# First tile of an attention and two-layer gated kernel: two weight blocks multiplied in plain fp32 instead of in split halves

## The chip, the cores and the metric

The kernel runs on one core of one Trainium2 chip. The metric is the device time of one execution in microseconds (us). Before the change three runs took 1025.25, 1028.63 and 1029.28 us (median 1028.63 us).

Engines are named as in the profile: PE is the matrix engine (PEld its weight loads), DVE the vector engine, ACT the scalar engine, POOL the general-purpose engine, SP the one that issues the DMAs.

## The reference

Three layers follow each other. Attention over keys and values that are averaged eight at a time, then two feed-forward layers with a product of two projections in the middle; 2304 tokens, 512 model columns, 1536 inner columns.

```python
# attention: k and v averaged over 8 neighbours, softmax(q k^T / 8) v
xn = x / sqrt(mean(x * x) + 1e-6) * rms_g
g = xn @ w_gate                      # 512 -> 1536
h = g * sigmoid(g) * (xn @ w_val)
x2 = h @ w_out                       # 1536 -> 512
out = ((x2 @ w_a) * (x2 @ w_b)) @ w_out2
```

All weights arrive as float64 and are turned into fp32 on the chip.

## The kernel before

The tokens of the first feed-forward layer are cut into five tiles (512, 256, 512, 512, 512 tokens), the 1536 inner columns into twelve weight blocks of 128. For each block and tile PE computes gate (`g`) and value (`v`), each as four matmul steps over the 512 model columns; ACT takes silu of the gate (line 812), DVE multiplies it by the value (`ht`, line 818), and PE adds the block's share of the output into four PSUM accumulators (`acc`, line 675). Of `g` and of `v` there is one PSUM bank each, so that a new gate waits for the silu of the last one, and a new value for the product `ht` of the last one.

A product of two fp32 tensors is made in one of two ways. *Split*: each operand is divided into a high part (rounded to fp32r, a cast on ACT) and a low part (the rest, a subtraction), and three fp32r matmuls per step give low x high, high x high and high x low. `split_w` (line 618) does it for a weight block: cast `wh` at line 621, subtraction `wl` at line 622 on POOL, or on DVE where the token carries an exclamation mark. `split_x` (line 625) does it for the tokens: cast `xh` at line 636, subtraction `xl` at line 637. *Direct*: one fp32 matmul per step on the operands as they are. The profile records one fp32 matmul as two. The output projection of the first tile and the whole second tile are direct (lines 675 and 654), everything else of the layers is split.

While the first tile is computed, the weights are still arriving. Each of the 36 weight parts of the first layer goes through a chain (`convert_steps`, line 575): DMA into one of four staging buffers `st`, two ACT operations (lines 590 and 591), two DVE operations (lines 597 and 600), one POOL addition (line 607). A staging buffer is free for the next DMA when the POOL addition is done. The attention of the first 512 tokens, the keys of the next batch (line 189, line 180) and the normalisation (a few small DVE operations at lines 478 to 493, then the scaling of x at line 529, once for each half of 256 tokens) run on the same engines.

In the first tile the first two weight blocks are computed in halves of 256 tokens, so that work can start when the first half of x is there. The jobs are numbered: jobs 0 and 1 are blocks 0 and 1 on the first half, jobs 2 and 3 the same blocks on the second half, jobs 4 to 13 are blocks 2 to 11 on all 512 tokens. What each engine does in which order is set by the table `FIRST` (line 32), a list of tokens that is worked off from left to right: `g2a` and `g2b` are the two halves of job 2's gate, `v2a`, `v2b` its value, `a2` its silu, `h2` its product `ht`, `o2` its output matmuls; `s3.1` splits part 1 (value) of block 3, `x0` and `x1` split the two halves of x, `c` converts a weight part, `l` loads one. A `-` or `=` ahead of a token puts its instructions behind the work listed before on its engine. After that a scheduler places the instructions; the order on each engine is fixed when the program is built.

Of the kernel before, what the change touches and what calls it, by code (L numbers as in the profile page):

```python
# [20 lines left out]
SLICE = 768  # L21
HALF = SLICE // 2
FINE = 2
DIRECT = 0

# [4 lines left out]
FIRST = """  # L32
=k0 -A0.0@att =k1 l -k2! k3 -l t0@att =A0.1@acc1 A0.2@att w0 =A0.5@acc0 =A0.6@acc3 =A0.7@acc3
-w1 A0.3 =A0.4 w2 t1 =A0.8 A1.0@att A1.1@acc0 A0.9! =c l =A1.2@v -V0.0@acc0 A1.5@acc2 -A1.3
-V0.1@acc1 c A1.6@acc3 s0.0 -V0.2@acc0,v A1.4! -V0.3@g,acc0 =A1.7@acc1 A1.8 A1.9 V0.4@acc2,att
=V0.5@att -c =V1.0@acc0 =V0.6 =V0.7@v =V1.1@g -x0! -g0a V1.2@att,acc3 =V1.3@acc2,acc1 c =g0b
-V1.4@acc0,att =l V1.5@acc2 =V1.6 =V1.7@acc0 s0.1! =c =x1 -a0 s1.0 =v0a =v0b -c =h0 =o0 -g1a
-g1b -s1.1! =c L0 -a1 A2.0 -g2a v1a =L1 -g2b p0 =p1! v1b =c s2.0! h1 =c =a2 =c g3a =c v2a =v2b
-h2 =c g3b =o1 a3 =p2 =o2 -v3a =v3b -s2.1 -h3 g4a g4b p3! -c a4 -v4a s3.0 =c -p4 -v4b s3.1! =c
=o3 =g5a =p5! =c =h4 c -c s4.0! -g5b -c -a5 s4.1! v5a -s5.0 v5b -h5 -g6a -o4 -g6b a6 -p6 -c  # L40
=v6a p7 -s5.1 =v6b -A2.1 -g7a -c =g7b -h6 =c =M0 -c =A2.2 =c -A2.3 =s6.1! =s6.0! -a7 o5 -c v7a
=c =A2.4 v7b s7.0! -h7 -g8a -g8b =a8 -o6 s7.1! c =v8a A2.5 c =s8.0 =p8 v8b =g9a -V2.0 g9b -h8
-a9 -o7 v9a =g10a -s9.0 v9b -c =s8.1 -h9 =c =V2.1 =o8 -V2.2 g10b =s9.1! -a10 -c V2.3 =v10a
-V2.4 -c v10b s10.0 g11a -g11b -h10 =a11 =V2.5 =c -s10.1 =c =o9 -g12a =c -v11a s11.0 =A3.0
=g12b -v11b h11 =a12 -V2.6 -v12a -g13a c -o10 A3.1 -v12b -o11 =g13b -s11.1 =A3.2 -A3.3 =M1
-h12 a13 -v13a -V2.7 -v13b =o12 -h13 =A3.4 =o13 =A3.5
""".split()
SECOND = """
A4.0 =r0 -r1 r2 -r3 r4 -r5 V3.0 r7 =r6 =r8 -V3.1 =V3.2 N0 =V3.3 A4.1 -N1
# [14 lines left out]
def attention_moe_moe2(  # L64
# [715 lines left out]
    def first_tile():  # L780
# [8 lines left out]
        def half(j, part, c0):  # L789
            f, cols, last = jobs[j]  # L790
            if f < DIRECT:
                terms = ((wf[0, f, part], xf_t[0]),)
# [529 lines left out]
```

## Time and profile before

| | us |
|---|---|
| median of three runs | 1028.63 |
| the profiled execution, its own time | 1028.68 |
| its span from the first to the last instruction | 1026.9 |
| PE busy in the span | 984.9 (96%) |
| DVE, ACT, POOL busy | 608.1, 437.9, 369.5 |

The profiled execution's time stands 1.8 us over its span and 0.05 us over the median. PE is busy nearly all the time from about 120 us on; in the first four of the page's forty slices (25.7 us each) it stands at 4, 9, 8 and 8 tenths, in the stretch in which the first weights are being converted. The split products of the first tile begin at 43.8 us.

### The profile page before, as it was taken

To read this page: it belongs to the slowest core of one execution; us is meant where nothing else is said; L and a number is where in the kernel's file an instruction comes from. 1 tells how busy PE (TensorE), PEld (TensorE's weight loads), DVE (VectorE), ACT (ScalarE), POOL (GpSimd) and SP (SyncE) were. 2 spreads that over 40 slices of the span, in tenths; PEclk is the share of its full clock that TensorE was granted. 3 is DMA by queue.
4 is the path that set the end of the run, shared out by engine and by line. 5 is a ranking of instruction groups with operands and counts; after the bars stand their busy time and mean duration, and the time that the engine had idled before them with its cause. 6 is when DMAs were issued, how large, how long until landed. Compare 5 with 4: busy or idle time off the path is not lost. (4 is left out here: it accounts for less than half of the span.)

```text
span 1026.9 us, 13276 instructions
## 1 busy us (share of the span) xinstructions
PE 984.9 (96%) x4820; PEld 845.0 (82%) x4820; DVE 608.1 (59%) x963; ACT 437.9 (43%) x822; POOL 369.5 (36%) x301
## 2 busy tenths in 40 slices
PE   4988999999999989999999999999999999999998
PEld 3776676778888877888788899999999998888886
DVE  6898966564733765363627759766776665322221
ACT  3845661232534545444445445434444434331211
POOL 6476672100153433443348620533344333310000
PEclk9889999999999999999999999999999999999999
DMA  8556543320100002000112133444443444643431
GB/s 227 156 175 194 178 140 105 102 78 1 41 1 21 1 1 62 1 1 1 41 28 75 42 111 113 139 148 135 140 151 125 130 129 178 203 140 118 139 113 72
DMA packets 82801, 101.53 MB, mean 99 GB/s; under 512 B 24112, under 2 KB 63024, under 8 KB 82736
## 3 DMA queue, kind: packets, MB, share of 16 engines
q1 hardware_dynamic: 82736, 100.69, 31.7%
q8 instruction: 38, 0.62, 0.2%
q14 instruction: 27, 0.22, 0.1%
HBM read 73.93 MB, written 26.74 MB: 98 GB/s over the span
## 5 line engine op out<-in xcount | busy, mean ns | idle before, releaser
L622 POOL TENSOR_TENSOR wl<-wf,wh 128x512 fp32r<-128x512 f32 x121 | 164.4, 1366 | 263.0 <-ACT wh L621 255.3
L621 ACT CAST wh<-wf 128x512 fp32r<-128x512 f32 x132 | 80.2, 619 | 76.2 <-PE acc L667 27.4
L1103 DVE TENSOR_TENSOR hl<-hf,hh 128x768 fp32r<-128x768 f32 x36 | 35.5, 992 | 95.1 <-ACT hh L1102 95.1
L1125 PE MATMUL o<-woh,hl 128*128 128x512 f32 x216 | 85.8, 397 | 0.0
L1125 PE MATMUL o<-woh,hh 128*128 128x512 f32 x216 | 85.0, 394 | 0.0
L1125 PE MATMUL o<-wol,hh 128*128 128x512 f32 x216 | 84.7, 392 | 0.0
L607 POOL TENSOR_TENSOR w<-w,st 128x512 int32<-128x512 int32 x24 | 31.9, 1330 | 116.0 <-DVE w L600 114.8
L1102 ACT CAST hh<-hf 128x768 fp32r<-128x768 f32 x36 | 29.8, 834 | 91.4 <-PE o L1125 81.5
L675 PE MATMUL acc<-ht,wf 128*128 128x256 f32 (+1 forms) x208 | 67.0, 465 | 1.2 <-DVE ht L818 0.7
L607 POOL TENSOR_TENSOR wf<-wf,st 128x512 int32<-128x512 int32 x36 | 52.9, 1475 | 39.0 <-DVE wf L600 17.3
L1240 ACT ACTIVATE ht<-g 128x512 f32<-128x512 f32 (+1 forms) x48 | 26.1, 544 | 92.8 <-PE g L654 90.2
L1248 DVE TENSOR_TENSOR ht<-ht,v 128x512 f32<-128x512 f32 (+1 forms) x48 | 29.6, 617 | 56.2 <-PE v L654 54.9
L667 PE MATMUL acc<-hh,wl 128*128 128x512 f32 x144 | 57.7, 400 | 3.5 <-ACT hh L1257 3.5
L654 PE MATMUL v<-xh,wl 128*128 128x512 f32 x144 | 57.9, 402 | 0.0
L667 PE MATMUL acc<-hl,wh 128*128 128x512 f32 x144 | 56.8, 394 | 0.1
L654 PE MATMUL g<-xh,wl 128*128 128x512 f32 x144 | 56.7, 394 | 0.0
L667 PE MATMUL acc<-hh,wh 128*128 128x512 f32 x144 | 56.6, 393 | 0.0
L654 PE MATMUL v<-xl,wh 128*128 128x512 f32 x144 | 56.3, 391 | 0.0
L654 PE MATMUL g<-xh,wh 128*128 128x512 f32 x144 | 56.2, 390 | 0.0
L654 PE MATMUL v<-xh,wh 128*128 128x512 f32 x144 | 56.1, 390 | 0.0
L654 PE MATMUL g<-xl,wh 128*128 128x512 f32 x144 | 56.1, 390 | 0.0
L1032 ACT COPY p<-X 128x384 f32<-128x384 f32 x36 | 17.3, 480 | 90.1 <-PE X L1024 90.1
(212 smaller groups left out, 2731.5 us busy)
## 6 DMA issues: line engine op xcount, KB each, us to landing
hf<-h SPq DMA_DIRECT2D x36, 384.0 KB
st<-in_moe_w_out_dram SPq DMA_DIRECT2D x24, 512.0 KB
h<-u SPq DMA_DIRECT2D x36, 192.0 KB
h<-p SPq DMA_DIRECT2D x36, 192.0 KB
st<-in_moe_w_gate_dram SPq DMA_DIRECT2D x12, 512.0 KB
st<-in_moe_w_val_dram SPq DMA_DIRECT2D x12, 512.0 KB
st<-in_moe_w_a_dram SPq DMA_DIRECT2D x12, 512.0 KB
st<-in_moe_w_b_dram SPq DMA_DIRECT2D x12, 512.0 KB
```

The costliest lines, as they stand in the source:

```text
L607: nc.gpsimd.tensor_tensor(out=bits, in0=bits, in1=low, op=ALU.add)
L621: nc.scalar.copy(wh, wf[ph, f, i])
L622: (nc.vector if boot["alt"] else nc.gpsimd).tensor_sub(wl, wf[ph, f, i], wh.bitcast(F32))
L654: nc.tensor.matmul(bank[:, :n], w[:, c, :], x[:, c, cols], start=(i == 0), stop=(i == len(terms) * KD - 1),)
L667: nc.tensor.matmul(accs[c][:, cols], w[:, c, :], x[:, :n], start=(f == 0 and i == 0 and cols.start == 0), stop=(f == NF - 1 and i == 2),)
L675: nc.tensor.matmul(accs[c][:, cols], wf[0, f, 2][:, c, :], ht[:, :cols.stop - cols.start], start=(f == 0 and cols.start == 0), stop=(f == ...
L1032: nc.scalar.copy(t, src[:, :HALF])
L1102: nc.scalar.copy(hh, hf)
L1103: nc.vector.tensor_sub(hl, hf, hh.bitcast(F32))
L1125: nc.tensor.matmul(accs[i], x[:, sub], y, start=(f == 0 and j == 0), stop=(f == NF - 1 and j == 2),)
L1240: act = nc.scalar.activation(out=ht[:, :m], in_=gb[:, :m], func=AF.Silu)
L1248: nc.vector.tensor_mul(ht[:, :m], ht[:, :m], vb[:, :m])
```

## The change

`DIRECT` goes from 0 to 2: gate and value of weight blocks 0 and 1 (jobs 0 to 3) are made directly, one fp32 matmul per step on `xf` and `wf`, in place of three fp32r matmuls. In the table the four tokens `s0.0`, `s0.1`, `s1.0`, `s1.1` (the splits of gate and value of these blocks) are taken out, and `x0!` and `x1`, which stood ahead of job 0's gate and among the tokens of job 0, now stand after job 2's silu, before block 2 needs them. The split of the output weights, of all other blocks and of all later tiles stays.

```diff
-DIRECT = 0
+DIRECT = 2
...
-=V0.5@att -c =V1.0@acc0 =V0.6 =V0.7@v =V1.1@g -x0! -g0a V1.2@att,acc3 =V1.3@acc2,acc1 c =g0b
+=V0.5@att -c =V1.0@acc0 =V0.6 =V0.7@v =V1.1@g -g0a V1.2@att,acc3 =V1.3@acc2,acc1 c =g0b
...
-g1b -s1.1! =c L0 -a1 A2.0 -g2a v1a =L1 -g2b p0 =p1! v1b =c s2.0! h1 =c =a2 =c g3a =c v2a =v2b
+A2.0 -g2a v1a =L1 -g2b p0 =p1! v1b =c s2.0! h1 =c =a2 =c -x0! g3a =c v2a =v2b =x1 -h2 =c g3b
```

The order on the engines moves at two places that matter below.

On PE, where the first gate begins (`g_401` and `v_513` before, `g_391` and `v_483` now, are gate and value of job 0; `kT` is a transpose for the next batch). Before:

```order
L434 MATMUL sq_1_413<-ones_100,sq_1_3_466 128x2 x2
L804 MATMUL g_401<-xh_395,wl0_288 128x256
L804 MATMUL g_401<-xh_395,wh0_287 128x256
L804 MATMUL v_513<-xh_395,wl1_494 128x256
L804 MATMUL v_513<-xh_395,wh1_493 128x256
L210 MATMUL kT_1_912<-ident_95,kp_1_605 128x72
L804 MATMUL g_401<-xl_396,wh0_287 128x256
L804 MATMUL g_401<-xh_395,wl0_288 128x256
```

Now:

```order
L434 MATMUL sq_1_399<-ones_100,sq_1_3_448 128x2 x2
L804 MATMUL g_391<-xf_0_292,wf0_0_0_240 128x256 x4
L804 MATMUL v_483<-xf_0_292,wf1_0_0_276 128x256 x4
L210 MATMUL kT_1_832<-ident_95,kp_1_543 128x72
L318 MATMUL sc_4_0_849<-KB0_106,qTs_4_528 64x144 x2
L804 MATMUL g_505<-xf_0_292,wf0_0_1_421 128x256
```

Gate and value of job 0 now stand as four matmuls each, in one piece, with the transpose behind them instead of among them.

On DVE, from the product `ht` of job 1 to that of job 2 (`ht_570` and `ht_642` before, `ht_520` and `ht_576` now). Before:

```order
L529 TENSOR_TENSOR xf_0_296<-xf_0_296,rb_1_490 128x4x256
L637 TENSOR_TENSOR xl_396<-xf_0_296,xh_395 128x2x256 x2
L818 TENSOR_TENSOR ht_570<-ht_570,v_590 128x256
L622 TENSOR_TENSOR wl0_630<-wf0_0_2_562,wh0_629 128x512
L597 TENSOR_SCALAR wf2_0_2_636<-wf2_0_2_636 128x512
L189 TENSOR_REDUCE kp_1_605<-kv_1_4_608 72x64
L600 SCALAR_TENSOR_TENSOR wf2_0_2_636<-st_0_2_2_526,wf2_0_2_636 128x512
L597 TENSOR_SCALAR wf0_0_3_646<-wf0_0_3_646 128x512
L818 TENSOR_TENSOR ht_642<-ht_642,v_667 128x256
```

Now:

```order
L622 TENSOR_TENSOR wl0_564<-wf0_0_2_512,wh0_563 128x512
L818 TENSOR_TENSOR ht_520<-ht_520,v_536 128x256
L597 TENSOR_SCALAR wf2_0_2_570<-wf2_0_2_570 128x512
L597 TENSOR_SCALAR wf0_0_3_580<-wf0_0_3_580 128x512
L600 SCALAR_TENSOR_TENSOR wf2_0_2_570<-st_0_2_2_488,wf2_0_2_570 128x512
L600 SCALAR_TENSOR_TENSOR wf0_0_3_580<-st_0_3_0_510,wf0_0_3_580 128x512
L637 TENSOR_TENSOR xl_587<-xf_0_292,xh_586 128x2x256 x2
L597 TENSOR_SCALAR wf1_0_3_597<-wf1_0_3_597 128x512
L637 TENSOR_TENSOR xl_587<-xf_0_292,xh_586 128x2x256
L600 SCALAR_TENSOR_TENSOR wf1_0_3_597<-st_0_3_1_555,wf1_0_3_597 128x512
L637 TENSOR_TENSOR xl_587<-xf_0_292,xh_586 128x2x256
L818 TENSOR_TENSOR ht_576<-ht_576,v_603 128x256
```

All four subtractions `xl`, two of which stood far earlier and two ahead of job 1's product, now stand between the products of jobs 1 and 2, with three conversions.

## Rows read from the trace of the kernel before

**Rows 1.** The page: busy time, share of the span and instructions of each engine.
```profile
PE 984.9 (96%) x4820; PEld 845.0 (82%) x4820; DVE 608.1 (59%) x963; ACT 437.9 (43%) x822; POOL 369.5 (36%) x301
```

**Rows 2.** Windows: stretch, length, busy us of each engine, granted clock, DMA.
```profile
43.78:58.65 14.87, 10.41 (x50) 8.86 (x50) 14.61 (x27) 8.01 (x15) 8.50 (x8) 0.73 0.53 158
58.65:76.62 17.97, 16.55 (x92) 14.84 (x92) 15.75 (x21) 10.93 (x20) 12.87 (x11) 0.87 0.56 180
76.62:116.44 39.82, 35.88 (x146) 25.91 (x147) 35.13 (x46) 23.09 (x39) 23.94 (x18) 0.96 0.64 199
116.44:1026.90 910.46, 894.39 (x4393) 772.60 (x4391) 510.59 (x807) 373.06 (x700) 299.80 (x229) 1.00 0.28 87
```

**Rows 3.** Timeline of PE: start, length, instruction, count, idle before it and releaser.
```profile
46.06 0.38 PE L210 MATMUL kT<-ident,kp 72*128 72x72 f32 x1 [1.06 <-DVE kp L189]
...
54.96 0.70 PE L472 MATMUL rb<-dg,ones 128*128 128x256 f32 x2 [1.99 <-DVE dg L464]
...
58.65 1.22 PE L675 MATMUL acc<-ht,wf 128*128 128x256 f32 x2 [0.52 <-DVE xf L529]
...
76.62 0.47 PE L804 MATMUL v<-xh,wl 128*128 128x512 f32 x1 [1.42 <-DVE ht L818]
...
86.86 0.64 PE L804 MATMUL v<-xh,wl 128*128 128x512 f32 x1 [2.77 <-DVE ht L818]
...
113.56 0.50 PE L804 MATMUL g<-xh,wl 128*128 128x512 f32 x1 [1.17 <-DVE wl L622]
```

**Rows 4.** Timeline of PE: split matmuls ten apart, first at 1.2, then at 2.4 GHz.
```profile
47.03 0.41 PE L804 MATMUL g<-xh,wl 128*128 128x256 f32 x1
...
49.17 0.41 PE L804 MATMUL v<-xh,wl 128*128 128x256 f32 x1
...
70.97 0.28 PE L804 MATMUL v<-xh,wh 128*128 128x256 f32 x1
...
72.17 0.28 PE L804 MATMUL v<-xl,wh 128*128 128x256 f32 x1
```

**Rows 5.** Timeline of PE: fp32 matmuls of 256 columns, at 1.2 and at 2.4 GHz.
```profile
26.63 1.91 PE L420 MATMUL xT<-ef,vm 128*128 128x256 f32 x4
28.34 0.45 PE L318 MATMUL sc<-KB,qTs 128*128 128x144 f32 x1
...
208.57 1.89 PE L654 MATMUL g<-xf,wf 128*128 128x256 f32 x8
210.30 0.38 PE L367 MATMUL eT<-ident,e 128*128 128x128 f32 x2
```

**Rows 6.** Timeline of DVE: the products `ht` of jobs 1, 2 and 4.
```profile
63.84 0.42 DVE L818 TENSOR_TENSOR ht<-ht,v 128x256 f32<-128x256 f32 x1 [1.56 <-PE v L804]
...
67.09 0.42 DVE L818 TENSOR_TENSOR ht<-ht,v 128x256 f32<-128x256 f32 x1
...
86.14 0.68 DVE L818 TENSOR_TENSOR ht<-ht,v 128x512 f32<-128x512 f32 x1
```

**Rows 7.** Groups of DVE from 63.8 to 94 us: count, busy us, mean ns.
```profile
L600 DVE SCALAR_TENSOR_TENSOR wf<-st,wf 128x512 int32<-128x512 int32 x11 | 12.9, 1174 | 0.2
L597 DVE TENSOR_SCALAR wf<-wf 128x512 int32<-128x512 int32 x11 | 9.0, 819 | 0.0
...
L189 DVE TENSOR_REDUCE kp<-kv 72x64 f32<-72x512 f32 x2 | 2.2, 1087 | 0.0
```

**Rows 8.** Timeline of DVE and POOL: the subtractions of x, and POOL beside one pair.
```profile
45.92 1.29 DVE L637 TENSOR_TENSOR xl<-xf,xh 128x512 fp32r<-128x512 f32 x2
...
59.28 3.01 DVE L637 TENSOR_TENSOR xl<-xf,xh 128x512 fp32r<-128x512 f32 x2 [0.69 <-ACT xh L636]
...
60.01 2.86 POOL L180 TENSOR_TENSOR kv<-kv 72x512 f32<-72x512 f32 x2
```

**Rows 9.** Timeline of DVE: a conversion's two operations with POOL idle.
```profile
33.57 0.42 DVE L597 TENSOR_SCALAR wf<-wf 128x512 int32<-128x512 int32 x1
34.02 0.69 DVE L600 SCALAR_TENSOR_TENSOR wf<-st,wf 128x512 int32<-128x512 int32 x1
```

More of the change, by code (lines that the diff above doesn't have):

```diff
@@ L34 @@
 -w1 A0.3 =A0.4 w2 t1 =A0.8 A1.0@att A1.1@acc0 A0.9! =c l =A1.2@v -V0.0@acc0 A1.5@acc2 -A1.3
--V0.1@acc1 c A1.6@acc3 s0.0 -V0.2@acc0,v A1.4! -V0.3@g,acc0 =A1.7@acc1 A1.8 A1.9 V0.4@acc2,att
-=V0.5@att -c =V1.0@acc0 =V0.6 =V0.7@v =V1.1@g -x0! -g0a V1.2@att,acc3 =V1.3@acc2,acc1 c =g0b
[L37 to L46, printed above, removed]
+-V0.1@acc1 c A1.6@acc3 -V0.2@acc0,v A1.4! -V0.3@g,acc0 =A1.7@acc1 A1.8 A1.9 V0.4@acc2,att
+=V0.5@att -c =V1.0@acc0 =V0.6 =V0.7@v =V1.1@g -g0a V1.2@att,acc3 =V1.3@acc2,acc1 c =g0b
+-V1.4@acc0,att =l V1.5@acc2 =V1.6 =V1.7@acc0 =c -a0 =v0a =v0b -c =h0 =o0 -g1a -g1b =c L0 -a1
+A2.0 -g2a v1a =L1 -g2b p0 =p1! v1b =c s2.0! h1 =c =a2 =c -x0! g3a =c v2a =v2b =x1 -h2 =c g3b
+=o1 a3 =p2 =o2 -v3a =v3b -s2.1 -h3 g4a g4b p3! -c a4 -v4a s3.0 =c -p4 -v4b s3.1! =c =o3 =g5a
+=p5! =c =h4 c -c s4.0! -g5b -c -a5 s4.1! v5a -s5.0 v5b -h5 -g6a -o4 -g6b a6 -p6 -c =v6a p7
+-s5.1 =v6b -A2.1 -g7a -c =g7b -h6 =c =M0 -c =A2.2 =c -A2.3 =s6.1! =s6.0! -a7 o5 -c v7a =c
+=A2.4 v7b s7.0! -h7 -g8a -g8b =a8 -o6 s7.1! c =v8a A2.5 c =s8.0 =p8 v8b =g9a -V2.0 g9b -h8 -a9
+-o7 v9a =g10a -s9.0 v9b -c =s8.1 -h9 =c =V2.1 =o8 -V2.2 g10b =s9.1! -a10 -c V2.3 =v10a -V2.4
+-c v10b s10.0 g11a -g11b -h10 =a11 =V2.5 =c -s10.1 =c =o9 -g12a =c -v11a s11.0 =A3.0 =g12b
+-v11b h11 =a12 -V2.6 -v12a -g13a c -o10 A3.1 -v12b -o11 =g13b -s11.1 =A3.2 -A3.3 =M1 -h12 a13
+-v13a -V2.7 -v13b =o12 -h13 =A3.4 =o13 =A3.5
 """.split()
```

## The prediction

> **What bounds the kernel now.** I read the page first, then the windows, then the timelines of PE and DVE where the windows show PE idle.
>
> The page shows PE busy for 96% of the span [rows 1]. The windows tell where the rest is: from 116.44 us to the end PE works 894.39 of 910.46 us, while in the three stretches from 43.78 to 116.44 us, where the first tile's split products stand, it works 62.8 of 72.7 us, and the granted clock is 0.73, 0.87 and 0.96 there [rows 2]. With two levels of the clock (1.2 and 2.4 GHz) a mean of 0.73 says that 54% of 14.87 us, 8.0 us, ran at 1.2 GHz, and 0.87 that 26% of 17.97 us did. The change works only in these stretches. Whatever it shifts at 116 us reaches the end nearly whole, since PE is the bound from there on; so the question is by how much PE gets past 116 us earlier or later.
>
> The timeline of PE names what it waits for in these stretches: keys on DVE (1.06 us at 46.06), the normalisation on DVE (1.99 us at 54.96, 0.52 us at 58.65), and the products `ht` and a `wl` on DVE (1.42, 2.77 and 1.17 us at 76.62, 86.86 and 113.56) [rows 3]. Each is DVE's. DVE is busy 14.61 of 14.87, 15.75 of 17.97 and 35.13 of 39.82 us there [rows 2]: until about 87 us the first tile runs at the pace of DVE's queue, not of PE. That decides how I count.
>
> **The change part by part.**
>
> *The products on PE.* At 1.2 GHz ten split matmuls take 2.14 us, at 2.4 GHz 1.20 us [rows 4]; a half tile's gate or value has twelve: 2.57 and 1.44 us. Direct it has four fp32 matmuls, eight records. Four records of that size take 1.71 us at 1.2 GHz (26.63 to 28.34), eight take 1.73 us at 2.4 GHz (208.57 to 210.30) [rows 5]: 3.42 and 1.73 us. So each of the eight products (gate and value of jobs 0 to 3) costs PE 0.85 us more at the lower level, 0.29 us at the higher: 2.3 us if all stand at 2.4 GHz, 6.8 us if none does, 4.6 us with half of them at each, as the clock of the first two stretches suggests. Where PE waits for DVE anyway this is hidden; it counts in full where a DVE operation waits for PE, which is the case at one point, job 1's `ht`.
>
> *What goes from ACT, POOL and DVE.* Four weight splits: four casts `wh` and two subtractions on ACT and POOL, two on DVE. ACT and POOL are busy for 8.01 and 8.50 of 14.87 us in the first stretch [rows 2], so I count nothing for theirs; if their queues carried the stretch, it would be up to their own 1 to 3 us, and that stands in the faster rival. On DVE one of its two subtractions and the first pair `xl` (1.29 us at 45.92 [rows 8]) stood ahead of the second half's scaling. A subtraction `wl` has the form of half such a pair, 0.65 us. So the scaling, and with it the second half of x on PE, comes 0 to 1.9 us earlier. I take 1.0, the middle, since job 0's `ht` also stands in DVE's queue there, and waits for PE products that are now longer.
>
> *Up to job 1's `ht`* (63.84 us; DVE had waited 1.56 us for PE [rows 6]). From 58.65 us PE had done one output matmul and twenty split matmuls for it, gate of job 2 and value of job 1 mixed; now the same place holds one output matmul and seven direct ones. At 1.2 GHz: 20 x 0.214 = 4.3 us against 7 x 0.855 = 6.0 us, 1.7 us more. With the 1.0 us from above, job 1's `ht` comes 0.7 us later (bounds -0.2 and +1.7).
>
> *From job 1's `ht` to job 2's.* This is where the moved split of x lands. Before, 3.25 us (63.84 to 67.09 [rows 6]). Now ten DVE operations stand ahead of job 2's `ht`: three L597, three L600 and four `xl`, after job 1's `ht` of 0.42 us. Bare, by 0.42 and 0.69 us [rows 9] and 0.645 us (half of the pair at 45.92 [rows 8]) this is 0.42 + 1.26 + 2.07 + 2.58 = 6.3 us. But beside POOL's work the same operations take longer: L600 1.17 and L597 0.82 us in the mean of the stage [rows 7], and a pair `xl` 3.01 us where POOL's two additions (2.86 us at 60.01) ran with it [rows 8]: 0.42 + 2.46 + 3.51 + 6.02 = 12.4 us. From both I take off 0.6 us: two operations of 0.69 us would take 1.38 and the pair takes 1.29, so that each starts about 0.08 us before the last one ends, at the seven that are not `xl`. Bounds 5.7 and 11.8 us. POOL is busy in about two thirds of the second and third stretch [rows 2], but two of its additions are gone too; I take 9.0 us, a little over the middle. So job 2's `ht` comes 5.7 us later against job 1's (2.5 to 8.5).
>
> The Trainium skill, in "GPSIMD Engine Reference" (1. Specifications), says that POOL and DVE share their SBUF interfaces, and that a DVE instruction with two SBUF inputs, or in a two-port mode, contends with POOL for them. The pair at 59.28 us agrees, at 3.01 against 1.29 us. By this rule every `xl` that meets a POOL addition waits, and this term would stand at its upper bound; without it at the lower.
>
> *From job 2's `ht` to job 4's.* Before 19.05 us (67.09 to 86.14 [rows 6]), in which DVE was the pace. In the new order two L600 and one L597 fewer stand there (they have moved ahead) and one more L189: -2 x 1.17 - 0.82 + 1.09 = -2.1 us by the means [rows 7], -0.7 us bare (0.69 and 0.42 [rows 9]). I take -1.9.
>
> *The sum.* Job 4's `ht`, for which PE waits at 86.86 us, comes 0.7 + 5.7 - 1.9 = 4.5 us later. PE alone would get there 4.6 us of work later, minus 1.06 us (job 0's gate and value no longer have the transpose and `xl` in their midst) and minus the waits of 1.42 and 2.77 us: -0.7 us. DVE comes later, so DVE decides. After that the work is the same; I let the wait of 1.17 us and the clock of the third stretch stand (0; -2.8 if both went, +1.7 for another 3.4 us at 1.2 GHz). 1028.68 + 4.5 = **1033.2 us**, against the profiled execution, which stands at the median.
>
> **The rivals.**
>
> *The bare queue.* DVE's new queue meets POOL seldom: -0.2 + 2.5 - 0.7 = +1.6, 1030.3 us. For it: POOL has two additions fewer, and DVE waits for PE before job 1's `ht`, time in which POOL can run ahead. Against: the means of rows 7 stand in just this stage.
>
> *Every subtraction collides.* +1.7 + 8.5 - 1.9 = +8.3, 1037.0 us. It decides as soon as POOL's `wl` subtractions of blocks 2 and 3 fall between jobs 1 and 2. For it: the pair of 3.01 us. Against: POOL would have to be busy without a break.
>
> *Faster, by PE as the pace.* If the weights get through DVE and POOL earlier by what is taken out, the queue is short when job 1 ends. Then the waits of 1.06, 1.42 and 2.77 us go, the slow part of the third stretch with them (8% of 39.82 us, 1.6 us lost), and the products cost 2.3 us at full clock: 2.3 - 1.06 - 1.42 - 2.77 - 1.6 = -4.6, 1024.1 us. It decides if job 4's `ht` comes by 86 us. For it: DVE loses 1.3 us of `wl` in all. Against: it keeps all four `xl` and gets them at its busiest place.
>
> **How the numbers follow.** A measurement of this kernel can tell 0.5%, 5.1 us, from no change. Forecast: 0.50, its own range 1030.7 to 1036.2, 0.20 of it above 1033.8. Bare queue 0.18, inside 0.5%. All colliding 0.22, slower. Faster 0.10, half of it by more than 0.5%. So slower 0.42, same 0.30 + 0.18 + 0.05 = 0.53, faster 0.05. The range takes in the bare queue, most of the colliding case and half of the faster one: 1027.2 to 1038.5 us.
>
> **What would show it.** Right: PE's gate and value of job 0 in one piece without the wait at 46 us; `ht` of job 1 within 2 us of 63.84; 7 to 11 us from there to job 2's `ht`, with `xl` pairs well over 1.3 us; a new wait of PE for that `ht` at its output matmuls; job 4's `ht` at about 90.6 us; the stretch after 116 us as long as before. Wrong: job 4's `ht` at 86 us or earlier, or PE without a wait for `ht` between 65 and 90 us (then the products alone are the cost), or a stretch after 116 us that gives the delay back.

## The result and the profile after

Twelve runs of the changed kernel took 1030.22 to 1038.05 us, median 1033.33; twelve of the kernel before, on the same chip, 1025.25 to 1029.73, median 1027.28. The ratio is 1.006, with a 95% interval of 1.0043 to 1.0077: 6 us slower. The profiled execution took 1031.21 us with a span of 1029.3, 2.1 us under its median. The forecast said 1033.2 us.

By the page PE is busy for 984.1 us of the span, before for 984.9 [rows 1]. The windows of the same first three stretches (answers [rows 2]; columns as there):

```profile
43.78:58.65 14.87, 11.53 (x41) 8.81 (x41) 14.28 (x26) 8.32 (x15) 9.72 (x9) 0.81 0.57 173
58.65:76.62 17.97, 14.14 (x56) 11.04 (x55) 14.54 (x18) 9.98 (x19) 11.74 (x9) 0.91 0.46 147
76.62:116.44 39.82, 36.25 (x156) 26.14 (x155) 35.24 (x49) 21.58 (x36) 26.11 (x18) 1.00 0.68 205
```

PE is busy for 14.14 us of the second stretch, before for 16.55. Its waits (answers [rows 3]):

```profile
53.48 1.56 PE L675 MATMUL acc<-ht,wf 128*128 128x256 f32 x6 [1.86 <-DVE ht L818]
...
56.52 0.70 PE L472 MATMUL rb<-dg,ones 128*128 128x256 f32 x2 [1.49 <-DVE dg L464]
...
68.63 0.50 PE L804 MATMUL g<-xh,wl 128*128 128x512 f32 x1 [1.05 <-ACT ht L812]
...
70.26 0.50 PE L804 MATMUL g<-xl,wh 128*128 128x512 f32 x1 [0.90 <-DVE xl L637]
...
72.89 3.45 PE L675 MATMUL acc<-ht,wf 128*128 128x256 f32 x8 [1.89 <-DVE ht L818]
...
88.90 0.50 PE L804 MATMUL v<-xh,wl 128*128 128x512 f32 x1 [1.57 <-DVE ht L818]
...
115.19 0.50 PE L804 MATMUL g<-xh,wl 128*128 128x512 f32 x1 [0.99 <-DVE wl L622]
```

The wait for keys at 46 us is gone. New are waits for job 0's `ht` (1.86), for the silu that frees the gate's bank (1.05, at job 4's first gate matmul), for an `xl` (0.90) and for job 2's `ht` at its output matmuls (1.89); these last three make 3.84 us. At job 4's `ht` PE waits 1.57 us, before 2.77.

DVE's timeline, the products of jobs 1, 2 and 4 (answers [rows 6]) and the subtractions `xl` (answers [rows 8]):

```profile
62.51 0.42 DVE L818 TENSOR_TENSOR ht<-ht,v 128x256 f32<-128x256 f32 x1 [3.43 <-ACT wf L590]
...
64.72 3.47 DVE L637 TENSOR_TENSOR xl<-xf,xh 128x512 fp32r<-128x512 f32 x2
...
71.82 0.68 DVE L637 TENSOR_TENSOR xl<-xf,xh 128x512 fp32r<-128x512 f32 x1
72.42 0.41 DVE L818 TENSOR_TENSOR ht<-ht,v 128x256 f32<-128x256 f32 x1
...
88.17 0.68 DVE L818 TENSOR_TENSOR ht<-ht,v 128x512 f32<-128x512 f32 x1
```

From job 1's to job 2's product it now takes 9.91 us, before 3.25, and an `xl` takes 0.68 us at 71.82 but 3.47 for the pair at 64.72, with POOL at work. Job 4's product comes 2.0 us later than before.

The next view wasn't among the rows of before: DVE in the normalisation of the second half, four of its small operations on four columns that met POOL, one that did not (46.26), and `dg`, and under them POOL in the same time. Job 0's product stands among them at 53.01.

```profile
46.26 0.15 DVE L491 TENSOR_TENSOR by<-br 128x4 f32<-128x4 f32 x1
...
46.67 1.24 DVE L492 TENSOR_TENSOR by<-by,ba 128x4 f32<-128x4 f32 x1
...
48.84 1.26 DVE L491 TENSOR_TENSOR by<-br 128x4 f32<-128x4 f32 x1
...
50.63 2.46 DVE L492 TENSOR_TENSOR by<-by,ba 128x4 f32<-128x4 f32 x1
...
54.00 1.54 DVE L492 TENSOR_TENSOR by<-by,ba 128x4 f32<-128x4 f32 x1
...
56.00 0.47 DVE L464 TENSOR_SCALAR dg<-ident,br 128x128 f32<-128x128 f32 x2
...
46.48 1.41 POOL L607 TENSOR_TENSOR wf<-wf,st 128x512 int32<-128x512 int32 x1 [6.56 <-DVE by L491]
48.65 1.43 POOL L607 TENSOR_TENSOR wf<-wf,st 128x512 int32<-128x512 int32 x1 [0.75 <-ACT st L591]
50.05 1.79 POOL L180 TENSOR_TENSOR kv<-kv 72x512 f32<-72x512 f32 x1
51.80 1.27 POOL L607 TENSOR_TENSOR wf<-wf,st 128x512 int32<-128x512 int32 x1
...
53.83 0.46 POOL L183 TENSOR_TENSOR kp<-kv 72x128 f32<-72x128 f32 x1
54.26 1.27 POOL L622 TENSOR_TENSOR wl<-wf,wh 128x512 fp32r<-128x512 f32 x1
```

The operation on four columns at 46.26 us, with POOL idle, takes 0.15 us. Against that L492 at 46.67 ends at 47.91, and POOL's addition at 47.89; L491 at 48.84 ends at 50.10, POOL's at 50.08; L492 at 50.63 ends at 53.09, the second of two POOL operations that follow each other without a gap at 53.07; L492 at 54.00 begins beside POOL's L183 and ends at 55.54, POOL's next operation, again without a gap, at 55.53. These four take 6.50 us in place of 0.6. The Trainium skill, in "SBUF — State Buffer" (Who interferes with whom), says that a DVE instruction with two inputs in SBUF contends with a POOL instruction that reads SBUF, through a port pair that the two engines share, and that this is an exclusive lock. The ends of these four agree with it to 0.02 us.

### The profile page after: what moved, and what is told of

Same layout as the page of the kernel before. It is cut to its first block, busy times and chain, and to the rows that moved or that the text cites. A ratio compares the mean times of both kernels' runs of the same rounds, so it can differ in the third digit from the quotient of the medians.

```text
span 1029.3 us, 13210 instructions
## 1 busy us (share of the span) xinstructions
PE 984.1 (96%) x4788; PEld 841.5 (82%) x4788; DVE 608.3 (59%) x961; ACT 435.5 (42%) x818; POOL 368.4 (36%) x299
## 5 line engine op out<-in xcount | busy, mean ns | idle before, releaser
L622 POOL TENSOR_TENSOR wl<-wf,wh 128x512 fp32r<-128x512 f32 x119 | 161.4, 1363 | 261.3 <-ACT wh L621 253.6
L621 ACT CAST wh<-wf 128x512 fp32r<-128x512 f32 x128 | 77.6, 618 | 82.2 <-PE acc L667 26.9
L675 PEld LDWEIGHTS acc<-ht,wf 128*128 128x128 f32 x208 | 39.7, 194 | 23.2 <-issue 14.6
```

The costliest lines, as they stand in the source:

```text
L621: nc.scalar.copy(wh, wf[ph, f, i])
L622: (nc.vector if boot["alt"] else nc.gpsimd).tensor_sub(wl, wf[ph, f, i], wh.bitcast(F32))
L675: nc.tensor.matmul(accs[c][:, cols], wf[0, f, 2][:, c, :], ht[:, :cols.stop - cols.start], start=(f == 0 and cols.start == 0), stop=(f == ...
```

## The experiments

All times are medians; the ratio is to the kernel before in the same series (its medians were 1027.4 to 1028.0 us), with its 95% interval. "Normalisation" is the time from L478, the first small operation of the second half, to the start of `dg`: 11.9 us in the changed kernel (44.07 to 56.00), 10.3 before (43.80 to 54.07). The kernel before, `dg` and the scaling on DVE:

```profile
54.07 0.83 DVE L464 TENSOR_SCALAR dg<-ident,br 128x128 f32<-128x128 f32 x2
...
57.38 1.21 DVE L529 TENSOR_TENSOR xf<-xf,rb 128x1024 f32<-128x1024 f32 x1
```

### The changed kernel again

No edit.

> The changed kernel once more, for a second profile and as the yardstick of the other runs. From its first runs: 1033.3 us, 6 us over the kernel before. The first profile was of an execution 2 us under its own median, and it lost only 3.4 us of time at the low clock after 50 us; if the median's missing 2 us are lost clock, this profile has one or two more slow stretches of 3.4 us (1.7 us each) between 50 and 130 us; if they are a longer queue on DVE, the product ht of job 4 comes later than 88.2 us at the same clock.

1034.43 us, ratio 1.0053 (1.0037 to 1.007). DVE's timeline (products of jobs 1, 2, 4), and the first three windows of [rows 2]:

```profile
66.41 0.42 DVE L818 TENSOR_TENSOR ht<-ht,v 128x256 f32<-128x256 f32 x1 [4.48 <-ACT wf L590]
...
76.32 0.41 DVE L818 TENSOR_TENSOR ht<-ht,v 128x256 f32<-128x256 f32 x1
...
92.09 0.67 DVE L818 TENSOR_TENSOR ht<-ht,v 128x512 f32<-128x512 f32 x1
```

```profile
43.78:58.65 14.87, 11.27 (x40) 8.66 (x40) 12.79 (x25) 9.67 (x17) 8.21 (x7) 0.73 0.52 154
58.65:76.62 17.97, 14.29 (x54) 11.07 (x53) 12.78 (x15) 8.36 (x16) 11.05 (x9) 0.88 0.50 143
76.62:116.44 39.82, 36.95 (x152) 26.76 (x153) 35.07 (x47) 21.37 (x36) 26.81 (x19) 0.96 0.61 185
```

The first answer is the right one: it is not a longer queue on DVE. The granted clock is 0.73, 0.88 and 0.96 in place of 0.81, 0.91 and 1.00, and job 4's product comes at 92.09, 3.92 us later. The normalisation takes 11.9 us in both profiles, and from job 1's product to job 4's it is 25.66 and 25.68 us. Of the 3.92 us, 1.73 lie ahead of the normalisation, which starts at 45.80 in place of 44.07, and 2.17 between PE's first `rb` matmul and job 1's product: 8.16 us (from 58.25) at a granted clock of 0.73 in place of 5.99 (from 56.52) at 1.00, and 0.73 over 8.16 us says 2.2 us lost at the lower level. One profile alone places nothing to better than that.

### Direct products alone

```diff
-DIRECT = 0
+DIRECT = 2
```

(in the kernel before; the four weight splits stay and are used by nothing)

> The table of the kernel before with DIRECT = 2: gate and value of jobs 0 to 3 are direct, but all splits of weights and of x stay where they were, the four weight splits unused. Theory Q (DVE's queue with the moved xl between the products of jobs 1 and 2 is the cost): DVE's queue is that of before, so about 1028 us (1027 to 1029.5). Theory P (the direct products themselves, 2.3 to 6.8 us of PE, are the cost): 1031 to 1034 us, as with the whole change.

1025.28 us, ratio 0.9977 (0.9968 to 0.9987): 2.4 us *faster* than before. Theory P falls; theory Q's price was too high as well. The windows of the kernel before and of this one, from the second half's first small operation to the end of job 1's product and to the end of job 4's:

```profile
43.80:64.25 20.45, 15.99 (x76) 14.13 (x76) 18.03 (x31) 9.81 (x18) 13.08 (x12) 0.69 0.50 149
...
43.80:86.81 43.01, 34.41 (x172) 29.59 (x172) 40.45 (x57) 24.81 (x45) 30.09 (x25) 0.85 0.57 176
```

```profile
43.55:58.18 14.63, 11.96 (x46) 9.37 (x47) 14.46 (x30) 10.14 (x19) 7.05 (x7) 0.90 0.46 144
...
43.55:85.45 41.90, 33.95 (x133) 27.17 (x134) 41.25 (x57) 25.16 (x45) 28.72 (x25) 0.88 0.58 182
```

In both, DVE begins 57 operations up to job 4's product. Job 1's product ends 14.63 us after the start in place of 20.45. Of these 5.8 us nearly nothing is won up to `rb` (11.17 us, before 11.16). From there to job 1's product it is 3.05 us in place of 8.88: PE now makes job 1's value in one piece directly behind `rb`. Behind job 1's product the same kernel is slow:

```profile
55.26 1.89 PE L804 MATMUL v<-xf,wf 128*128 128x256 f32 x8
...
69.23 3.78 PE L675 MATMUL acc<-ht,wf 128*128 128x256 f32 x8 [4.54 <-DVE ht L818]
```

```profile
59.31 5.22 DVE L597 TENSOR_SCALAR wf<-wf 128x512 int32<-128x512 int32 x2
```

Job 2's product comes 11.01 us after job 1's, with only one pair `xl` (1.28 us) in between; two L597 (bare 0.42 us each [rows 9]) take 5.22 us while POOL runs without a gap from 58.93 to 64.24, and PE waits 4.54 us for job 2's product. And yet this kernel has the lowest ratio of all: neither the length of this stretch nor PE's waits in it are a price by themselves.

### x split later, or earlier

```diff
-h1 =c =a2 =c -x0! g3a =c v2a =v2b =x1 -h2 =c g3b
+h1 =c =a2 =c g3a =c v2a =v2b h2 -x0! =c =x1 g3b
```

> The changed kernel with the split of x placed behind the product of job 2 in place of ahead of it; PE then no longer has four gate matmuls of job 4 ahead of job 2's output matmuls. Theory Q in its narrow form (the cost is job 2's ht being late): job 2's ht about 4 us after job 1's in place of 9.9, PE's wait of 1.9 us for it gone, 1028 to 1030 us. Theory T (it is the sum of DVE's work from job 1's to job 4's ht, wherever the xl stand in it): job 4's ht again at about 88 us, 1032 to 1034 us. Theory P (products): 1032 to 1034 us as well, but with PE busy without the waits for ht.

1032.66 us, ratio 1.0042 (1.0025 to 1.0059). The products of jobs 1, 2 and 4:

```profile
64.90 0.42 DVE L818 TENSOR_TENSOR ht<-ht,v 128x256 f32<-128x256 f32 x1 [3.43 <-ACT wf L590]
...
68.55 0.41 DVE L818 TENSOR_TENSOR ht<-ht,v 128x256 f32<-128x256 f32 x1
...
89.51 0.68 DVE L818 TENSOR_TENSOR ht<-ht,v 128x512 f32<-128x512 f32 x1
```

Job 2's product follows 3.65 us after job 1's, and yet nearly nothing is won: narrow Q falls, T holds. What stood ahead of job 2's product stands ahead of job 4's now.

```diff
-p0 =p1! v1b =c s2.0! h1 =c =a2 =c -x0! g3a =c v2a =v2b =x1 -h2
+x0! x1 p0 =p1! v1b =c s2.0! -h1 =c =a2 =c g3a =c v2a =v2b -h2
```

> The changed kernel with all four xl ahead of job 1's product, where DVE stood idle for 3.4 us in the changed kernel (59 to 62.5 us). Theories Q and T: the xl leave the crowded stretch, job 2's ht comes about 4 us after job 1's, job 4's ht 2 to 4 us earlier than 88.2 us, 1028 to 1030 us. Theory P: 1032 to 1034 us. If the xl delay the scaling of the second half instead, job 1's ht comes after 64 us and the gain is lost there: 1031 to 1033 us.

1030.53 us, ratio 1.0018 (1.0007 to 1.0029). DVE, `dg` and the product of job 1:

```profile
58.09 0.48 DVE L464 TENSOR_SCALAR dg<-ident,br 128x128 f32<-128x128 f32 x2
...
65.15 0.41 DVE L818 TENSOR_TENSOR ht<-ht,v 128x256 f32<-128x256 f32 x1
```

Some 3.6 us are won, where Q and T had expected 4.4 to 6.4, and the normalisation is 12.2 us long (45.92 to 58.09). The sign of the third case came too: job 1's product stands after 64 us, and two of the `xl` (57.49 and 58.49 us) stand ahead of the scaling at 59.69. So the place behind job 1 costs something, and something else remains. From the three traces I formed a theory N: with the splits and the `xl` gone from DVE's and POOL's front, the scheduler moves later conversions up into the normalisation, and POOL's additions of these hold up its small operations.

### The square: splits kept or gone, x early or late

With direct products in all four, two corners were missing. One is the changed kernel with x split where it was:

```diff
-=V1.1@g -g0a
+=V1.1@g -x0! -g0a
...
-=c -a0
+=c =x1 -a0
...
-=c -x0! g3a =c v2a =v2b =x1 -h2
+=c g3a =c v2a =v2b -h2
```

> The four weight splits gone as in the changed kernel, x split where the kernel before splits it. With the kernel that keeps the splits and the place of x (direct products alone: 1025.3 us) and the changed kernel (1034.4 us) it makes a square of two by two. Theory Q (the late place of the xl): about 1025.5 us. Theory N (with the splits gone, later conversions move up into the normalisation of the second half, and POOL's additions of these hold up DVE's small operations there: 11.9 us from the first of them to dg in the changed kernel, 9.2 us with the products alone): normalisation of 11 to 12 us again and 1029 to 1032 us.

The other is the direct products alone, all splits kept, with the opposite edit (`x0!` and `x1` to where the change has them):

> The other corner of the square: direct products, the four weight splits kept (unused), x split at the place of the changed kernel. Theory Q: about 1033 us, as the changed kernel, since all four xl and three conversions stand between the products ht of jobs 1 and 2. Theory N: normalisation 9 to 10.5 us, job 0's ht at 50 to 51 us, and 1026 to 1029 us.

| ratio to before | x where it was | x where the change has it |
|---|---|---|
| weight splits kept | 0.9977 (0.9968 to 0.9987) | 1.0045 (1.0033 to 1.0057) |
| weight splits gone | 1.0002 (0.9991 to 1.0013) | 1.006 and 1.0053 |

In microseconds (times 1027.3): the direct products give 2.4 us; moving x costs 7.0 with the splits and 5.2 to 6.0 without; taking the splits out costs 2.6 with x at its old place and 0.8 to 1.5 with x at the new one, where the intervals overlap and no cost is shown. With x at its old place, useless work removed made the kernel slower. The larger part of the loss comes with the moved x. Neither theory named both corners: Q missed the one (1027.61 us against 1025.5), N the other (1031.15 against 1026 to 1029). In the kernel with x moved and the splits kept the normalisation is 9.85 us, with the direct products alone 9.24, so its length is not the loss there. PE's waits ahead of job 2's output matmuls, the last piece of job 1's value, and job 1's product on DVE:

```profile
59.28 1.03 PE L804 MATMUL v<-xf,wf 128*128 128x256 f32 x4
...
69.72 0.80 PE L804 MATMUL g<-xh,wl 128*128 128x512 f32 x1 [4.23 <-ACT ht L812]
...
73.99 3.78 PE L675 MATMUL acc<-ht,wf 128*128 128x256 f32 x8 [1.40 <-DVE ht L818]
```

```profile
60.42 0.42 DVE L818 TENSOR_TENSOR ht<-ht,v 128x256 f32<-128x256 f32 x1 [4.20 <-ACT wh L621]
```

With another 0.42 us for an `xl` at 71.36 these are 6.05 us of waits, 3.84 in the changed kernel and 4.54 at the same place with the direct products alone. By stages, x moved against the direct products alone: up to `dg` 0.6 us more, from there to job 1's product 3.1 (8.12 against 4.98), to job 2's 2.1 (13.10 against 11.01), to job 4's 0.3 less. The largest of these stands ahead of the queue that the forecast counted. With x at its old place PE makes job 1's value in one piece (55.26 us above; 60.63 with the splits gone); with x moved it makes it in two pieces with job 2's gate and an output product between, the last one ends at 60.31, and DVE stands idle for 4.20 us ahead of the product. In the changed kernel the value is cut up too (58.35 to 62.41 us), and DVE stands idle for 3.43. No run changed this order alone, so its price isn't shown.

### The hold

```diff
--c =h0 =o0
+h0 -c =o0
```

(in the changed kernel: job 0's product holds the next conversion behind it; one conversion in place of three then stands ahead of it on DVE, and the product itself stands behind `dg`)

> The changed kernel with two of the three conversions that moved ahead of job 0's product held behind it (its product placed without the minus, one conversion marked behind it); the xl stay late. Theory N: the small operations of the normalisation meet fewer POOL additions, it takes 8 to 9.5 us in place of 11.9, job 0's ht comes at 50 to 51 us, the scaling of the second half 2 to 3 us earlier than 57.3 us, and the time is 1029 to 1031 us. Theory Q: the queue between jobs 1 and 2 is the same, so 1033 to 1034.5 us.

1027.3 us, ratio 1.0001 (0.9987 to 1.0016). The whole loss is gone, with all four `xl` where the change has them. DVE (`dg`, the product of job 2), PE's wait for job 2, and the window to the end of job 1's product, here and in the changed kernel:

```profile
51.77 0.48 DVE L464 TENSOR_SCALAR dg<-ident,br 128x128 f32<-128x128 f32 x2
...
71.10 0.41 DVE L818 TENSOR_TENSOR ht<-ht,v 128x256 f32<-128x256 f32 x1
```

```profile
71.57 1.99 PE L675 MATMUL acc<-ht,wf 128*128 128x256 f32 x8 [0.80 <-DVE ht L818]
```

```profile
45.24:62.19 16.95, 13.61 (x53) 10.64 (x53) 14.68 (x28) 7.85 (x14) 10.18 (x9) 0.90 0.39 126
```

```profile
44.07:62.92 18.85, 15.51 (x59) 12.24 (x59) 15.12 (x28) 12.30 (x23) 12.47 (x11) 0.86 0.53 162
```

The normalisation takes 6.5 us (45.24 to 51.77), job 1's product ends 16.95 us after its start in place of 18.85 (21.0 in the second profile), and from job 1's product to job 2's it is still 9.3 us. N had expected too little.

The same hold in the kernel before, as a control:

> The kernel before with the same hold (job 0's product without its minus, a conversion behind it). If the hold is a gain of its own that has nothing to do with the change, this stands 4 to 7 us under the kernel before, at 1020 to 1023 us, as the changed kernel with the hold stands 6 us under itself. If the hold only takes back what the change let in, it is within 2 us of the kernel before: 1025.5 to 1029 us.

1027.97 us, ratio 1.0 (0.999 to 1.001). `dg` on DVE:

```profile
48.80 1.04 DVE L464 TENSOR_SCALAR dg<-ident,br 128x128 f32<-128x128 f32 x2
```

The hold is no gain of its own. But it shortens the normalisation here as well, from 10.3 to 6.5 us (42.28 to 48.80), and nothing is won by it. So the length of the normalisation is not a price by itself, and the hold alone doesn't show by which way it takes the loss back.

### Three additions left out

```diff
+if box["key"][:3] not in ((0, 1, 1), (0, 1, 2), (0, 2, 0)):
     nc.gpsimd.tensor_tensor(out=bits, in0=bits, in1=low, op=ALU.add)
```

(in the changed kernel; the low words of three weight parts are not added)

> The changed kernel without POOL's additions of the low words for three weight parts (value and output of block 1, gate of block 2), those that in the changed kernel run between 46 and 53 us beside the normalisation of the second half; DVE's order up to job 2's product stays, the conversions and the xl among them. Theory N in the form 'POOL's additions hold up DVE's small operations': normalisation 8 to 10 us in place of 11.9, job 0's ht 2 to 3 us earlier, time 1028 to 1031 us. If the conversions cost by their own place in DVE's queue (3 x 1.1 us), the normalisation stays over 11 us and the time at 1032 to 1034 us.

1028.91 us, ratio 1.0012 (1.0 to 1.0024). DVE in the normalisation, the last operation ahead of job 0's product and `dg`:

```profile
52.29 0.16 DVE L492 TENSOR_TENSOR by<-by,ba 128x4 f32<-128x4 f32 x1
...
53.70 0.47 DVE L464 TENSOR_SCALAR dg<-ident,br 128x128 f32<-128x128 f32 x2
```

DVE's order is that of the changed kernel up to `dg`, the three conversions included, L492 is back at 0.16 us at 52.29, and the normalisation (46.02 to 53.70) takes 7.7 us in place of 11.9. So what lengthens it is POOL's work beside it and not the conversions' own place on DVE; besides the three additions, a `wl` subtraction that POOL runs there in the changed kernel (54.26 us) is not there either, the first one now comes at 59.37. The 4.25 us pass on in full to job 1's product, which starts 14.19 us after the normalisation's start in place of 18.44. So the gain lies there, and not in staging buffers that come free earlier behind it. The ratio falls by 0.0041 to 0.0048, 4.2 to 4.9 us. What makes up the 1.2 us that are left over the kernel before wasn't taken apart.

### Towards a faster one

```diff
-=V1.1@g -g0a
+=V1.1@g -x0! -g0a
...
--c =h0 =o0
+h0 =x1 -c =o0
...
-=c -x0! g3a =c v2a =v2b =x1 -h2
+=c g3a =c v2a =v2b -h2
```

(in the changed kernel)

> The same hold, with the x split early: its first half ahead of job 0's gate, its second half ahead of job 1's product, and two conversions behind job 0's product; the weight splits gone. Both theories take their cause away: 1023 to 1026 us, at or under the direct products alone (1025.3). If it stands above 1028 us, neither names the cause.

1027.08 us, ratio 0.9994 (0.9983 to 1.0005): with the hold, x split early or late makes no difference that can be told (1.0001 and 0.9994). The 1023 to 1026 us that both theories expected were not reached.

```diff
-DIRECT = 0
+DIRECT = 2
...
--c =h0 =o0
+h0 -c =o0
```

(in the kernel before)

> Direct products with all splits at their old places, and the hold: the candidate for the fastest. In the kernel without the hold one conversion stands in the normalisation (9.2 us); with it none does, so 7 to 8 us, and 1022 to 1025 us if job 4's product still follows from there. If the held conversions only come late for block 1's output and block 2's gate, 1025 to 1027 us.

1027.21 us, ratio 0.9993 (0.9984 to 1.0002): above both ranges. The normalisation is 6.8 us long in place of 9.2, and nothing is won; the direct products alone stand 1.6 us lower without the hold, with intervals that just overlap.

```diff
--h2 =c g3b
+-h2 -s0.2 =c g3b
...
-    split_w(ph, f, 2)
+    if (2, f) not in ws:
+        split_w(ph, f, 2)
```

(in the kernel with the hold and the early x)

> The kernel with the hold and the early split of x (1027.1 us), and one more placement: the split of block 0's output weights, which no job of the first tile uses, stands behind job 2's product in place of wherever POOL has room. In every kernel without the four weight splits POOL ran it beside the first half's normalisation, which took 6.6 us there and 5.1 us in every kernel with them. If that is the rest of what the removed splits cost, the first normalisation takes 5.4 to 5.8 us and the time is 1 to 2 us lower, 1025 to 1026 us, level with the direct products alone (1025.3). If the 1 us is hidden behind PE's work of that stage, 1026.5 to 1027.5 us.

1027.01 us, ratio 0.9997 (0.9984 to 1.001). The first half's normalisation, from its first small operation at 35.17 us to `dg` at 40.78, takes 5.6 us as expected, against 6.6, and nothing is won: this microsecond was hidden. Of all kernels run, the direct products alone, with every split where it was, is the only one whose interval lies wholly under 1.

## Why the prediction came out right, step by step

**The products.** The price was right: the eight records of job 0's gate take 3.55 us (43.90 to 47.45) against 3.42, eight at the higher level 1.73 (63.10 to 64.83) as forecast, and job 0's gate and value stand in one piece, without the wait at 46 us. That PE's price is hidden was right too, and more than that: alone the products bring job 1's product 5.8 us forward and gain 2.4 us. The forecast counted a loss of 1.7 us at that point.

**The removed splits.** This step was incomplete. I counted the removed operations of ACT, POOL and DVE as nothing, but for a scaling that comes 1.0 us earlier (0 to 1.9). The places that they and the `xl` left did not stay empty. Three conversions in place of two stood ahead of job 0's product, POOL's additions ran beside the small operations, and the normalisation grew by 1.6 us. The run with three additions left out shows that POOL's work there costs the changed kernel 4.2 to 4.9 us; the hold takes back all of the loss, but its control leaves open how. The length of the normalisation doesn't order the kernels: it is 6.5 us with the hold in the kernel before (1027.97 us), 9.85 with x moved (1031.15) and 12.2 with x split earlier (1030.53). The order of instructions, read for the two places I had chosen, showed the `xl`; the additions in POOL's order I had not laid beside the normalisation.

**Up to job 1's product.** Forecast 0.7 us later (-0.2 to +1.7); 1.3 earlier in the first profile and 2.6 later in the second. Counted from the second half's first small operation it is 1.6 us less and 0.6 more than before. In the forecast's own two terms: the scaling was to come 1.0 us earlier and came 0.4 earlier and 0.1 later by this count (13.19 and 13.71 us after the start, before 13.58); a conversion that stood between `dg` and the scaling before (1.91 and 0.69 us from 54.83) makes up for the longer normalisation. PE's stretch from the scaling to job 1's product was to be 1.7 us longer and was 1.2 shorter and 0.4 longer.

**From job 1's to job 2's.** Forecast 9.0 us (5.7 to 11.8); 9.91 in both profiles, `xl` of 1.77 us among them. The queue is as described. What it costs isn't: with the hold it stands there at 9.3 us and costs nothing that can be told; split later it leaves this place and nearly the whole loss remains; and with the direct products alone the stretch takes 11.01 us in the kernel with the lowest ratio. DVE's operations up to job 4's product are 57 before and after, though not the same ones (one conversion more, one `wl` and one reduction of keys fewer). That a late product in their midst only matters where DVE or PE stands idle for it is how I read this; no run shows it by itself.

**From job 2's to job 4's.** Forecast 17.15 us; 15.75 and 15.77.

**Job 4's product, and the sum.** Forecast 90.6 us; 88.17 and 92.09, mean 90.1. The point to which the sum was made is the right one: in the fourteen profiles of all kernels job 4's product starts between 83.8 and 92.1 us, and the execution's time stands 939.3 to 943.0 us above that. Against the kernel before, the delay lies where the forecast put it: from job 1's product to job 4's 25.66 us in place of 22.30, 3.4 more, forecast 3.8. Against the direct products alone it lies elsewhere: up to job 1's product 4.2 and 6.4 us more, from there to job 4's 1.4 less. So the forecast had the place and the size of the difference between the two kernels, and missed that the products gain ahead of it and that the rest of the change takes this gain back. That the two cancel is luck. So is the agreement to 0.1 us: 4.5 us were added to 1028.68, the median of twelve runs of the kernel before is 1027.28, and the measured difference is 6.05.

**After 116 us.** Nothing was to be given back. At 113.56 us [rows 3] PE was 1.63 us behind; by the transposes of the queries at 218.44 us (217.77 before) it was 0.67. At the end of this profile it is 2.4 (a span of 1029.3 against 1026.9), since the clock fell once more, in the window

```profile
870.00:880.00 10.00, 8.96 (x35) 7.67 (x36) 6.65 (x10) 5.16 (x8) 4.82 (x4) 0.83 0.78 273
```

where 0.83 over 10 us says 3.4 us at the lower level, 1.7 us lost. In the second profile nothing was given back: 5.95 us at job 4's product, 6.0 at the end. That the clock stays as it was held for the second profile (0.73, 0.88, 0.96 against 0.73, 0.87, 0.96 [rows 2]) and not for the first.

**The rivals.** The bare queue and the general collision bounded the right term, but a collision that it didn't count, of the small operations, cost 4.2 to 4.9 us. The rule of the Trainium skill that I weighed ("GPSIMD Engine Reference", 1. Specifications) bore on the case more than I let it: it names DVE instructions with two SBUF inputs and sets no size, and I asked it only of the large ones. "Faster, by PE as the pace" comes near the time of the direct products alone (1024.1 against 1025.28 us), but not by its reason: nothing is taken out there, and PE still waits 2.40 us for `dg` and 4.54 for job 2's product.

What stays open: why the moved x costs 7.0 us with the splits kept and nothing that can be told with the hold. From job 1's product to job 2's it is 13.10 us in the one and 9.32 in the other; the `xl` take 5.89 and 4.86 us of that, a pair of L597 3.95 and 2.03. With the hold PE waits 0.80 us for job 2's product, but also 2.48 for a silu at 62.67. Job 1's value is in two pieces in both. The effects don't add: splitting x early wins 3.6 us, the hold 6, both together no more.

## What to carry to other kernels

Where a scheduler fills the queues, work that is removed is replaced by other work: ask what moves up into the gap and beside which chain it then runs. Look first at chains of many short DVE operations: the one here took 11.9 us beside POOL's work and 7.7 with three additions left out. And a late operation in a queue, or a long wait for it, is not yet a delay of the end: name a later point that the time follows, as job 4's product here, and compare the kernels there.

## What the runs showed of the hardware

In the changed kernel four DVE operations of 0.15 us that met POOL ended within 0.02 us of the end of a POOL operation. Of which one varies: those at 50.63 and 54.00 us waited through two POOL operations that follow without a gap (2.46 and 1.54 us), that at 48.84 only for the first, though POOL's next one begins at 50.05. An operation with one tensor input waited too: the two L597 of 5.22 us at 59.31 with the direct products alone. When the turn passes to DVE isn't shown. The other surprise is the scatter of one program: by the windows' granted clocks some 9 us at the lower level in one profile and 15 in the other between 43.78 and 116.44 us (5.7 + 3.2 and 8.0 + 4.3 + 3.2), with spans 3.6 us apart.
